# Closing the first expert tile two batch pairs before the end of attention, and rearranging the bridge around it

## The chip, the cores and the metric

The kernel runs on one core of a Trainium2 chip. The core has five engines with instruction queues of their own: TensorE (PE in the profile, with PEld for its weight loads), VectorE (DVE), ScalarE (ACT), GpSimd (POOL) and SyncE (SP, which here only issues transfers). Each queue runs in the order in which it was written, and the engines wait for one another by semaphores. The metric is the time of one execution on the device in microseconds (us), taken as the median over several runs; lower is better.

## The reference

The computation is a sliding-window attention followed by a mixture-of-experts layer without dropped tokens.

```python
# attention: batch 8, heads 8, sequence 576, head size 64, window 64, causal
scores = scale * np.matmul(q, k.transpose(0, 1, 3, 2))
scores = np.where(mask, scores, -1000000000.0)
attn = np.exp(scores - np.max(scores, axis=-1, keepdims=True))
attn = attn / (np.sum(attn, axis=-1, keepdims=True) + 1e-09)
out = np.matmul(attn, v)                      # reshaped to x: 4608 tokens x 512
# experts: 8, hidden size 1024
logits = x @ w_gate
expert_idx = np.argmax(logits, axis=1)        # one expert per token
gate_w = probs[np.arange(N), expert_idx]      # softmax of the logits, its largest entry
for e in range(E):                            # tokens sorted by expert
    h = np.maximum(x_sorted[lo:hi] @ w1[e], 0.0)
    y_sorted[lo:hi] = h @ w2[e]
return gate_w[:, None] * y[inv_perm]
```

So every token goes through one expert, and which one is known only when its attention output and its logits are done.

## The kernel before

**Attention.** The batch is cut into four pairs (`bg` 0 to 3, `last` = 3) and the heads into four pairs, which gives 16 units. A unit has three steps of three 128-token blocks each, so there are N = 48 steps, 0 to 47. `step(s)` writes out one step of a software pipeline by hand: PE computes the scores of step s + 1 into banks 0 and 1 (`scored`, L572), DVE masks them and takes the largest (`masked`, L585), ACT takes the exponentials (`softened`, L595); PE then does the weighted sum over v of step s - 1 in bank 6 (`weighted`, L618), part of the logits of step s - 3 (`logit`, L655), and turns the probabilities of step s (`flipped`, L603), which DVE and ACT copy (L605); DVE divides (`divided`, L628 to L632); PE turns q and k for step s + 3 (`turned`, L531 and L539) and the result of step s - 2 (`x_turned`, L643). Four banks (2 to 5) are handed out in a ring for what is turned. Other work is put behind these with a list, `todo[s]`, whose entries are written out in order at the end of step s.

**Routing.** When a pair's logits are complete, `by_tokens` brings them to token order and `choose(bg)` does the routing in five parts on DVE, with an exponential on ACT and two small matmuls: the largest logit (L686 to L692), the one-hot of the expert (L695, L698, exponential L699), the ranks among the tokens (L705) and the gate (L715 to L717), the running count (L722 to L732), and the position split in a high and a low part (L734 to L742). After that `place(j)` writes two one-hot matrices of the low part for each of the pair's nine blocks on DVE (L746), `weigh` scales a block by its gates (L757 on POOL, L755 on ACT), and `store` writes the result to `x_dram` (L766, L773). For the third pair (`bg` = 2) the function `after` lays this over steps 39 to 44: the five parts in steps 39, 39, 40, 41, 41, the one-hots three to a step in 42 to 44, the scalings in 41 to 44 with two of the nine on ACT, and in step 45 `first_tiles`.

**First tiles.** A tile holds 256 tokens of one expert. The first two tiles of expert 0 (`NE` = 2) are closed before the last pair is routed: `first_tiles` compares the high parts with the slot numbers of both tiles (L859, L862), multiplies the one-hots of 27 blocks in 54 narrow matmuls on PE (L869), takes the slots as token numbers (L872) and gathers tile 0's tokens on POOL (`gather_first`: a clear L280 and an indirect transfer L282 for each half). A count is raised to 512 for expert 0 after the third pair (L730), so that both tiles are padded if there are too few tokens.

**The bridge.** After step 47 the last pair's routing runs on DVE, and tile 0 goes through expert 0 as PE's filling between its parts: `turn` (eight transposes, L303, in banks 2 and 3, copies on ACT), `sums_x` (four DVE operations, L311), then `hidden` and `output` (fourteen block products, L322 and L362, in a Strassen scheme with seven for each layer). Sums of w2's blocks for that scheme are formed on POOL (`sums_w2`, four operations, L139, into the memory that held the turned q and k). `slot_table` builds the remaining slots from all 36 blocks: large comparisons (L799), the last nine blocks' one-hots and 72 narrow matmuls (L807). `next(tile0)` and `next(table)` alternate by hand. Tile 1 follows, then a loop over the experts that is bound by PE.

Memory of the q and k ring is used again: xg, the gathered rows, lies where unit 13's q was, and w2 of expert 0 lies where units 14 and 15 were, so its two halves are loaded from SP as those come free (L919).

Of the kernel before, what the change touches and what calls it, by code (L numbers as in the profile page):

```python
# [12 lines left out]
BF16 = mybir.dt.bfloat16  # L13
# [18 lines left out]
def _inner(ap: bass.AP, n: int) -> bass.AP:  # L32
    return _ins(ap, len(ap.ap), n)
# [3 lines left out]
def kernel(  # L37
# [174 lines left out]
    key = rt.tile([P, NJE], BF16, name="key")  # L212
    hi_e = rt.tile([P, NJE, NE * C], BF16, name="hi_e")
    at_b = rt.tile([P, NJ], BF16, name="at_b")
# [61 lines left out]

    def gather_first(tokens):

        for c in range(C):
            G.memset(xg[c], 0.0)  # L280

            G.indirect_dma_start(  # L282
                out=xg[c], out_offset=None, in_=x_dram[0 : NT - BG * S, :],
                in_offset=bass.IndirectOffsetOnAxis(ap=tokens[:, c : c + 1], axis=0),
                bounds_check=NT - BG * S - 1, oob_is_err=False,
            )
# [11 lines left out]

    def turn():
# [7 lines left out]
    def sums_x():  # L307

        b12, b22, b21 = tps[1][:, 0:HG], tps[1][:, HG:], tps[0][:, HG:]
        for n, (a, b) in enumerate(((b12, xq[:, 0, 0]), (b22, xs[:, 0]), (b22, xq[:, 0, 1]), (xs[:, 1], b21))):  # L310
            V.tensor_tensor(out=xs[:, n], in0=a, in1=b, op=ALU.subtract)  # L311
# [128 lines left out]
    with tc.manual_schedule(), ExitStack() as held, ExitStack() as brief:  # L440
# [236 lines left out]
        def choose(bg):  # L677
# [101 lines left out]
        def slot_table(hi):  # L779
# [53 lines left out]
        def after(s, routing, bg):  # L833
# [13 lines left out]

            for n in (0, 0, 1, 2, 2):
                do(n, part)
            for m in range(NTB):  # L850
                do(3 + m // 3, partial(place, bg * NTB + m))
                do((2, 2, 3, 3, 4, 4, 4, 5, 5)[m], partial(weigh, bg, m, nc.scalar if m in (2, 6) else G))
                if m % ST == ST - 1:
                    do(3 + m // ST, partial(store, bg, m // ST, G))
            do(6, first_tiles)

        def first_tiles():

# [3 lines left out]
            V.tensor_tensor(  # L862
                out=hi_e[:], in0=_inner(key[:], NE * C), in1=_ins(hi_id[:, C + 1 : C + 1 + NE * C], 1, NJE),
                op=ALU.is_equal,
            )
            slots = banks[next(tr_ring)](0, NE * C)
            for j in range(NJE):
                for i in range(2):
                    nc.tensor.matmul(  # L869
                        slots, lhsT=lo[:, i, j], rhs=hi_e[:, j], start=(i + j == 0), stop=(i + j == NJE)  # L870
                    )
            V.tensor_scalar(out=perm_e[:], in0=slots, scalar1=-1.0, scalar2=float(NT), op0=ALU.mult, op1=ALU.add)  # L872
            gather_first(perm_e[:, 0:C])

# [65 lines left out]
        tile0 = chain(hidden(0), turn(), output(0))  # L940
# [12 lines left out]
        next(by_tok[0], None)  # L953
        next(by_tok[1])
# [33 lines left out]
        gather(perm_i[:, 3 * C : 4 * C])  # L988
# [82 lines left out]
```

## Time and profile before

| | us |
|---|---|
| median of 7 runs | 765.42 |
| lowest, highest | 763.85, 766.90 |
| profiled execution, its own time | 764.96 |
| span of that profile | 763.1 |
| PE busy in the span | 721.1 (94%) |
| DVE, ACT, POOL busy | 397.0, 268.1, 357.0 |
| PE busy, 160 to 196 | 34.34 of 36 |
| PE busy, 196 to 214 | 12.94 of 18 |
| PE busy, 214 to 248 | 32.68 of 34 |
| PE busy, 248 to 763 | 491.71 of 515 |

The four stretches are: the steps in which the third pair is routed, the last attention steps, the bridge, and the expert tiles. In an answer in order of time, the columns are start, duration, engine, line, operation, what is written and read, count, and in brackets the idle time just before and what ended it. In the table by windows, the columns after the window are its length and then the busy time (and instructions) of PE, PEld, DVE, ACT and POOL, the granted TensorE clock as a share of the full one, the busy share of the transfer engines, and GB/s.

### The profile page before, as it was taken

Reading aid. Unit: us, or ns where it says so; the run is one execution under the profiler, and the core shown is the slowest. Engines: PE = TensorE matmul, PEld = TensorE weight load, DVE = VectorE, ACT = ScalarE, POOL = GpSimd, SP = SyncE. Lnnn points to the kernel's source line nnn. Section 1 sums busy time; section 2 is a strip of 40 time slices with the busy share of each in tenths; the row PEclk is TensorE's granted clock in tenths of the full one; section 3 lists DMA queues with packets and bytes.
Section 4 is the critical chain, followed back from the end, with each engine's and each line's share of the span. In section 5 each row is a group of like instructions: output and inputs, shape, how many; then the busy total and the mean of one; then the engine's idle time right before and its main releaser. Section 6 shows DMA issues by size and latency. Waiting matters only on the chain. (4 is left out here: it accounts for less than half of the span.)

```text
span 763.1 us, 18401 instructions
## 1 busy us (share of the span) xinstructions
PE 721.1 (94%) x7018; PEld 650.9 (85%) x7018; DVE 397.0 (52%) x1355; ACT 268.1 (35%) x676; POOL 357.0 (47%) x366
## 2 busy tenths in 40 slices
PE   5999999999799999999999999999999999999995
PEld 3888888887688988988999899899988899988994
DVE  2667898988758544523542353352434452424432
ACT  4788888787633201211221122111220121211220
POOL 4215567594760635537531653663256465262111
PEclk9999999999999999999999999999999999999998
DMA  7898889883513712603410260442171171101101
GB/s 158 208 212 190 187 195 253 178 222 122 191 45 125 277 58 61 234 29 136 161 53 33 92 212 29 159 149 70 30 255 46 39 256 56 42 24 42 43 29 53
DMA packets 137620, 94.55 MB, mean 124 GB/s; under 512 B 117072, under 2 KB 117072, under 8 KB 137490
## 3 DMA queue, kind: packets, MB, share of 16 engines
q1 hardware_dynamic: 127858, 62.16, 29.8%
q0 software_dynamic: 9056, 28.58, 11.6%
q10 hardware_dynamic: 576, 2.10, 0.8%
q8 instruction: 78, 1.28, 0.7%
q14 instruction: 52, 0.43, 0.2%
HBM read 73.94 MB, written 20.45 MB: 124 GB/s over the span
## 5 line engine op out<-in xcount | busy, mean ns | idle before, releaser
L322 PE MATMUL bank<-qk_m,s 128*128 128x128 f32 x1216 | 145.3, 275 | 0.0
L322 PEld LDWEIGHTS bank<-qk_m,s 128*128 128x128 f32 x1216 | 140.4, 192 | 0.0
L322 PE MATMUL bank<-qk_m,w 128*128 128x128 f32 x912 | 112.2, 276 | 12.6 <-DVE v_m L358 8.7
L272 POOL DMA_INDIRECT qk_m<-x_dram,at_g x42 | 44.6, 1063 | 168.3 <-PE bank L303 161.0
L322 PEld LDWEIGHTS bank<-qk_m,w 128*128 128x128 f32 x912 | 106.7, 192 | 17.6 <-issue 17.4
L595 ACT ACTIVATE pr<-pr,mx 128x128 f32<-128x128 f32 x288 | 89.7, 390 | 33.7 <-DVE mx L585 33.5
L358 DVE TENSOR_TENSOR v_m<-bank,v_m 128x256 f32<-128x256 f32 x101 | 40.9, 422 | 110.0 <-PE bank L362 54.8
L585 DVE CUSTOM_DVE_ANT_0 pr<-bank,mask 128x128 f32<-128x128 f32 x288 | 64.4, 286 | 27.4 <-PE bank L572 26.0
L329 ACT COPY qk_m<-bank 128x512 f32<-128x512 f32 x19 | 11.1, 586 | 166.0 <-PE bank L322 164.9
L292 POOL DMA_INDIRECT out_dram<-v_m,at_s x42 | 42.4, 1009 | 56.7 <-DVE v_m L358 44.9
L139 POOL TENSOR_TENSOR s<-w 128x1024 f32<-128x1024 f32 x22 | 52.3, 2377 | 18.4 <-DMA qk_m<-x_dram,at_g 14.3
L362 PE MATMUL bank<-qkT_m,v_m 128*128 128x256 f32 x240 | 54.0, 380 | 1.8 <-DVE v_m L139 1.8
L362 PEld LDWEIGHTS bank<-qkT_m,v_m 128*128 128x128 f32 x240 | 45.4, 190 | 8.7 <-DVE v_m L139 2.6
L362 PE MATMUL bank<-qk_m 128*128 128x256 f32 x224 | 52.1, 380 | 0.0
L513 POOL COPY v_m<-v_m 64x520 f32<-64x520 f32 x32 | 19.8, 619 | 68.0 <-DMA v_m<-in_v_dram 59.9
L618 PEld LDWEIGHTS bank<-v_m,pT 128*64 128x64 f32 x1152 | 41.1, 140 | 11.9 <-DVE xs L632 5.7
L618 PE MATMUL bank<-v_m,pT 128*64 128x65 f32 x1152 | 47.8, 231 | 2.9 <-DVE xs L632 2.9
L362 PE MATMUL bank<-s,v_m 128*128 128x256 f32 x216 | 48.1, 379 | 0.0
L572 PE MATMUL bank<-qkT_m 64*64 64x128 f32 x1152 | 46.0, 290 | 0.3 <-DVE mx L585 0.2
L362 PEld LDWEIGHTS bank<-qk_m 128*128 128x128 f32 x224 | 41.5, 190 | 5.5 <-ACT v_m L374 0.4
L362 PEld LDWEIGHTS bank<-s,v_m 128*128 128x128 f32 x216 | 41.0, 190 | 5.6
L539 PE MATMUL bank<-ident,qk_m 128*128 128x128 f32 x256 | 35.9, 283 | 7.9 <-POOL mask L461 4.9
(167 smaller groups left out, 1223.1 us busy)
## 6 DMA issues: line engine op xcount, KB each, us to landing
w<-in_moe_w_dram SPq DMA_DIRECT2D x11, 2048.0 KB, 14.8
qk_m<-in_q_dram SPq DMA_DIRECT2D x72, 128.0 KB, 3.5
qk_m<-in_k_dram SPq DMA_DIRECT2D x72, 128.0 KB, 3.6
v_m<-in_v_dram SPq DMA_DIRECT2D x64, 128.0 KB, 4.1
qk_m<-in_moe_w_dram SPq DMA_DIRECT2D x3, 2048.0 KB, 15.6
x_dram<-xs POOLq DMA_DIRECT2D x6, 512.0 KB, 4.5
x_dram<-xs POOLq DMA_DIRECT2D x3, 768.0 KB, 7.0
w<-in_moe_w_dram ACTq DMA_DIRECT2D x4, 512.0 KB, 4.1
```

The source lines that it names most:

```text
L139: op()
L272: G.indirect_dma_start(out=xg[c], out_offset=None, in_=x_dram[:, :], in_offset=bass.IndirectOffsetOnAxis(ap=at_g[:, c : c + 1], axis=0),)
L292: put = G.indirect_dma_start(out=out[:, :], out_offset=bass.IndirectOffsetOnAxis(ap=at_s[:, c : c + 1], axis=0), in_=ys[c], in_offset=None ...
L322: nc.tensor.matmul(acc[:, f, :], lhsT=a[:, g, f * P : (f + 1) * P], rhs=b[:, g, :], start=(first and f == 0 and g == 0), stop=(g == HG - 1 ...
L358: plus = lambda out, a, b: V.tensor_tensor(out=out, in0=a, in1=b, op=ALU.add)
L362: nc.tensor.matmul(acc, lhsT=a[:, f, :], rhs=b[:, f, :], start=(start and f == 0), stop=(stop and f == HF - 1), skip_group_check=True,)
L513: nc.gpsimd.tensor_copy(out=vb[0:D, i].rearrange("p j h d -> p (j h d)"), in_=va[D:P, i].rearrange("p j h d -> p (j h d)"),)
L539: nc.tensor.transpose(out=tr.rearrange("d a b -> d (a b)").rearrange("d (p j) -> d j p", j=NV)[:, j, :], in_=t[:, c, j].rearrange("p h d - ...
L572: nc.tensor.matmul(out_, lhsT=qT[rows, t, a * WINDOW : (a + 1) * WINDOW], rhs=rhs, start=True, stop=True, skip_group_check=True,)
L585: V.tensor_tensor_reduce(out=prs[h][:, m, :], in0=scs[h][:, m, :], in1=mask[:, m0 + m, :], scale=-scale, scalar=-2 * MASKED, op0=ALU.add, ...
L595: nc.scalar.activation(out=y, in_=y, func=AF.Exp, scale=-1.0, bias=mx[:, h, m : m + 1])
L618: nc.tensor.matmul(px[a * D : (a + 1) * D, h, m, :], lhsT=pTs[h][:, m, a * D : (a + 1) * D], rhs=vt[:, h, :], start=True, stop=True, skip_ ...
```

## The change

The selection of the first tiles is split. `first_tile(0)` works on the 18 blocks of the first two pairs, with its comparison in step 38 and its matmuls and gather in step 39; `first_tile(1)` works on 27 blocks and is written between the products of the bridge. The count of expert 0 is raised to 256 after the second pair and to 512 after the third. Tile 0 is turned in step 46 through banks 0 and 1, and its first product is written in step 47, with the sums of w2 behind it. The third pair's five parts move to steps 39, 40, 40, 41, 42, its one-hots to two each in 43 to 45 and three in 46, its scalings to steps 41 to 45, all on POOL. The loads of w2 stand one step earlier. In the bridge, 54 of the slot table's matmuls come behind the second three one-hots, and the last three scalings with their store come behind the copy of tile 0's first output product.

```diff
-            if bg == last - 1:
+            if last - NE <= bg < last:
-                V.tensor_scalar_max(count[:, 0:1], count[:, 0:1], float(NE * TB))
+                V.tensor_scalar_max(count[:, 0:1], count[:, 0:1], float((bg - last + NE + 1) * TB))
...
-            for j in range(NJE):
-                fill(j)
             for n in range(NST):
                 for m in range(ST):
                     place(NJE + n * ST + m)
+                if n == 1:
+                    for j in range(NJE):
+                        fill(j)
                 yield
...
-            for n in (0, 0, 1, 2, 2):
+            for n in (0, 1, 1, 2, 3):
                 do(n, part)
             for m in range(NTB):
-                do(3 + m // 3, partial(place, bg * NTB + m))
-                do((2, 2, 3, 3, 4, 4, 4, 5, 5)[m], partial(weigh, bg, m, nc.scalar if m in (2, 6) else G))
+                do((4, 4, 5, 5, 6, 6, 7, 7, 7)[m], partial(place, bg * NTB + m))
+                do((2, 3, 3, 4, 4, 5, 5, 6, 6)[m], partial(weigh, bg, m, G))
                 if m % ST == ST - 1:
-                    do(3 + m // ST, partial(store, bg, m // ST, G))
-            do(6, first_tiles)
-        def first_tiles():
+                    do(4 + m // ST, partial(store, bg, m // ST, G))
+        def first_tile(n):
+            nj = (last - NE + n + 1) * NTB
             V.scalar_tensor_tensor(
-                out=key[:], in0=rkhi[:, 0:NJE], scalar=1.0, in1=oh_all[:, 0, 0:NJE], op0=ALU.add, op1=ALU.mult
+                out=key[:, 0:nj], in0=rkhi[:, 0:nj], scalar=1.0, in1=oh_all[:, 0, 0:nj], op0=ALU.add, op1=ALU.mult
             )
...
+            yield
+            slots = banks[next(tr_ring)](0, C)
+            for j in range(nj):
                 for i in range(2):
                     nc.tensor.matmul(
...
+            to = perm_e[:, n * C : (n + 1) * C]
+            V.tensor_scalar(out=to, in0=slots, scalar1=-1.0, scalar2=float(NT), op0=ALU.mult, op1=ALU.add)
+            gather_first(to, nj * P)
+            yield
...
-        for n, s in enumerate((N - 6, N - 3)):
+        for n, s in enumerate((N - 7, N - 4)):
...
+        tile0 = chain(hidden(0), turn(), output(0))
+        first = first_tile(0)
+        todo.setdefault(N - 10, []).append(partial(next, first))
+        todo.setdefault(N - 9, []).append(partial(next, first))
+        free = [banks[i](0, NG, P) for i in (0, 1)]
+        todo.setdefault(N - 2, []).extend((lambda: form_all(turn(free)), partial(sums_x, free)))
+        todo.setdefault(N - 1, []).extend((partial(next, tile0), partial(sums_w2, 0)))
         for s in range(-3, N):
             step(s)
-        sums_w2(0)
...
         px = weighted(N - 1, pTs.pop(N - 1))
-        form_all(turn())
         logit(N - 3)
         divided(N - 1, px)
         x_turned(N - 2)
-        sums_x()
-        gather_first(perm_e[:, C : 2 * C])
+        second = first_tile(1)
+        next(second)
+        next(tile0)
         by_tok = [by_tokens(last, c) for c in range(NST)]
         next(by_tok[0])
-        next(tile0)
         logit(N - 2)
         x_turned(N - 1)
+        next(second)
...
         weigh_some(1)
-        next(tile0)
         next(routing, None)
-        weigh_some(2)
         next(tile0)
...
-        for _ in range(8):
+        for n in range(8):
             next(tile0)
             next(table, None)
+            if n == 1:
+                weigh_some(2)
```

More of the change, by code (lines that the diff above doesn't have):

```diff
@@ L212 @@
     key = rt.tile([P, NJE], BF16, name="key")
-    hi_e = rt.tile([P, NJE, NE * C], BF16, name="hi_e")
+    hi_e = rt.tile([P, NJE, C], BF16, name="hi_e")
     at_b = rt.tile([P, NJ], BF16, name="at_b")
@@ L275, in gather, with gather_first @@
             )
-    def gather_first(tokens):
+    def gather_first(tokens, rows):
         for c in range(C):
@@ L282, in gather_first @@
             G.indirect_dma_start(
-                out=xg[c], out_offset=None, in_=x_dram[0 : NT - BG * S, :],
+                out=xg[c], out_offset=None, in_=x_dram[0:rows, :],
                 in_offset=bass.IndirectOffsetOnAxis(ap=tokens[:, c : c + 1], axis=0),
-                bounds_check=NT - BG * S - 1, oob_is_err=False,
+                bounds_check=rows - 1, oob_is_err=False,
             )
@@ L297, in scatter, with turn @@
             tc.add_to_no_dep_group("puts", put.ins)
-    def turn():
+    def turn(tps=tps):
         for c in range(C):
@@ L305, in turn, with sums_x @@
         yield
-    def sums_x():
+    def sums_x(tps=tps):
         b12, b22, b21 = tps[1][:, 0:HG], tps[1][:, HG:], tps[0][:, HG:]
@@ L846, in after @@
                 return
-            for n in (0, 0, 1, 2, 2):
+            for n in (0, 1, 1, 2, 3):
                 do(n, part)
             for m in range(NTB):
-                do(3 + m // 3, partial(place, bg * NTB + m))
-                do((2, 2, 3, 3, 4, 4, 4, 5, 5)[m], partial(weigh, bg, m, nc.scalar if m in (2, 6) else G))
+                do((4, 4, 5, 5, 6, 6, 7, 7, 7)[m], partial(place, bg * NTB + m))
+                do((2, 3, 3, 4, 4, 5, 5, 6, 6)[m], partial(weigh, bg, m, G))
                 if m % ST == ST - 1:
-                    do(3 + m // ST, partial(store, bg, m // ST, G))
-            do(6, first_tiles)
-        def first_tiles():
+                    do(4 + m // ST, partial(store, bg, m // ST, G))
+        def first_tile(n):
+            nj = (last - NE + n + 1) * NTB
             V.scalar_tensor_tensor(
-                out=key[:], in0=rkhi[:, 0:NJE], scalar=1.0, in1=oh_all[:, 0, 0:NJE], op0=ALU.add, op1=ALU.mult
+                out=key[:, 0:nj], in0=rkhi[:, 0:nj], scalar=1.0, in1=oh_all[:, 0, 0:nj], op0=ALU.add, op1=ALU.mult
             )
             V.tensor_tensor(
-                out=hi_e[:], in0=_inner(key[:], NE * C), in1=_ins(hi_id[:, C + 1 : C + 1 + NE * C], 1, NJE),
-                op=ALU.is_equal,
-            )
-            slots = banks[next(tr_ring)](0, NE * C)
-            for j in range(NJE):
+                out=hi_e[:, 0:nj], in0=_inner(key[:, 0:nj], C),
+                in1=_ins(hi_id[:, (n + 1) * C + 1 : (n + 2) * C + 1], 1, nj), op=ALU.is_equal,
+            )
+            yield
+            slots = banks[next(tr_ring)](0, C)
+            for j in range(nj):
                 for i in range(2):
                     nc.tensor.matmul(
-                        slots, lhsT=lo[:, i, j], rhs=hi_e[:, j], start=(i + j == 0), stop=(i + j == NJE)
+                        slots, lhsT=lo[:, i, j], rhs=hi_e[:, j], start=(i + j == 0), stop=(i + j == nj)
                     )
-            V.tensor_scalar(out=perm_e[:], in0=slots, scalar1=-1.0, scalar2=float(NT), op0=ALU.mult, op1=ALU.add)
-            gather_first(perm_e[:, 0:C])
+            to = perm_e[:, n * C : (n + 1) * C]
+            V.tensor_scalar(out=to, in0=slots, scalar1=-1.0, scalar2=float(NT), op0=ALU.mult, op1=ALU.add)
+            gather_first(to, nj * P)
+            yield
         N = NU * NST
@@ L934 @@
         assert not todo
-        sums_w2(0)
         tr_ring = cycle((4, 5))
-        tile0 = chain(hidden(0), turn(), output(0))
         px = weighted(N - 1, pTs.pop(N - 1))
-        form_all(turn())
         logit(N - 3)
```

## The prediction

> **What bounds the kernel now.** Times are us from the start of the span, unless a sum says otherwise. The page first: PE is busy 94% of 763.1 us, and only a bridge, between the attention steps and the expert loop, has holes that the diff can reach. I then read the two-microsecond windows from 180 to 262, the waits of PE, and the order of time on PE, DVE and POOL there.
>
> ```profile
> 200.00:202.00 2.00, 0.38 (x4) 0.20 (x3) 1.97 (x16) 1.44 (x5) 1.71 (x2) 1.00 0.17 68
> 202.00:204.00 2.00, 0.93 (x37) 0.93 (x37) 0.95 (x4) 1.15 (x4) 2.00 (x4) 1.00 0.47 131
> 204.00:206.00 2.00, 2.00 (x49) 1.65 (x45) 0.16 (x1) 0.00 (x0) 0.08 (x1) 0.65 0.85 274
> 206.00:208.00 2.00, 2.00 (x32) 1.57 (x30) 1.35 (x12) 1.55 (x6) 0.79 (x1) 0.50 0.00 0
> 208.00:210.00 2.00, 1.27 (x12) 0.97 (x9) 1.28 (x4) 1.18 (x4) 1.73 (x3) 1.00 0.44 117
> ```
>
> PE (first pair after the window's length) stands nearly still from 200.4 to 203.1 and then runs at a granted clock of 0.65 and 0.50 for some 4 us (third value from the end).
>
> ```profile
> 188.06 0.55 PE L643 MATMUL bank<-ident,xs 128*128 128x128 f32 x3 [1.41 <-DVE pT L605]
> 203.07 1.49 PE L869 MATMUL bank<-hi_e,lo 128*128 128x4 bf16 x54 [2.70 <-DVE hi_e L862]
> 204.50 1.52 PE L572 MATMUL bank<-qkT_m 64*64 64x128 f32 x24
> 213.49 0.97 PE L618 MATMUL bank<-v_m,pT 128*64 128x65 f32 x24 [0.88 <-DVE xs L632]
> 240.05 1.91 PE L807 MATMUL bank<-hi,lo 128*128 128x62 bf16 x54 [1.29 <-DVE qk_m L311]
> 247.06 0.69 PE L807 MATMUL bank<-hi,lo 128*128 128x62 bf16 x18
> ```
>
> The releaser is DVE nearly each time. 213.49 is the weighted sum of the last step, 47: from there the last pair's routing starts. 247.06 are the last slots; tile 1's first product follows at 247.58 and PE is then full. So the change is worth what it moves 247.58.
>
> ```profile
> 192.98 0.81 DVE L746 TENSOR_SCALAR lo<-lane,low,tok_b 128x128 bf16<-128x128 bf16 x1
> 233.80 0.69 DVE L139 TENSOR_TENSOR v_m<-qk_m 128x512 f32<-128x512 f32 x1 [0.67 <-ACT qk_m L350]
> 261.82 2.84 DVE L139 TENSOR_TENSOR v_m<-qk_m 128x512 f32<-128x512 f32 x1 [0.76 <-ACT qk_m L350]
> ```
> ```profile
> 191.29 0.82 POOL L766 DMA_DIRECT2D x_dram<-xs  x1 [8.08 <-issue]
> 192.16 4.71 POOL L757 TENSOR_SCALAR xs<-xs,gate 128x512 f32<-128x512 f32 x3
> 210.19 2.36 POOL L139 TENSOR_TENSOR qkT_m<-qk_m 128x1024 f32<-128x1024 f32 x1
> ```
>
> These decide my forecast. A DVE subtraction takes 0.69 us alone and 2.84 while POOL runs its own L139; a one-hot takes 0.31 alone, 0.81 beside POOL's scalings (three tokens' pairs of them: 2.41 us from 192.76 to 195.17, against 1.34 alone). POOL idles 8.08 us before 191.29, and its sums of w2 run at 210.19, after all of the third pair's one-hots.
>
> **The change part by part.** The chip's later work is the same: by the reference's inputs expert 0 has 421 tokens in two pairs (256 needed) and 538 in three (512 needed), so no tile is padded.
>
> *Step 45's selection goes.* Off PE: the 2.70 wait, its 54 narrow matmuls (1.43, 203.07 to 204.50) and the half clock (scores 1.45 for 0.81, weighted sum 1.55 for 0.90, logits 0.57 for 0.35: 1.5). Together 5.6 us.
>
> *Tile 0's selection in steps 38 and 39.* 36 matmuls of 27 ns, 1.0 us, on a PE without a hole there. DVE's three small operations (0.2 each, by L859, L862, L872) lie beside it. POOL: two clears of 0.55 and two gathers of about 1.07 with 0.27 before each, 3.8 us, behind the copies that end at 179.06. So the scalings start at 182.9 instead of 180.10. The gather lands 3.4 us later, twenty before step 46 wants it.
>
> *Turn and first product in steps 46 and 47.* 1.04 and 1.88 us of PE move ahead of 213.49; tile 0's own work is not changed in sum. The turn must wait for the masking of step 47's scores (same banks 0, 1) and the product for all four sums of x (L311, 1.53).
>
> *Choosing one part per step.* In step 40 the gate now waits for an exponential that stands behind ACT's copy ending at 180.41: 180.41 + 0.27, then 0.73 of gate: masking starts at 181.45, was 180.34. Each step takes DVE 1.27 masking + 0.47 copy + 0.88 division = 2.62. To step 45's one-hots are five of these, 13.1, with part four (1.41), part five (1.28) and four one-hot pairs (0.89 + 0.89): 17.6 alone, so they are asked for at 199.0. But POOL, idle there before, now scales all nine blocks from 182.9 (the two that were ACT's, 0.74 each, too, which spares ACT nothing it lacked): 9 x 1.56 + stores 0.82 + 1.32 + 1.92 + 0.3 before each = 19.0, to 202.0. With two operations in 0.8, as in the 2.41 row, these extras become 2.4 + 2.3 + 1.6 + 1.6 and the one-hots are asked for at 202.5. Bounds 199.0 and 202.5; I take the middle, 200.8, as stores and gaps between scalings let operations through.
>
> *Sums of w2.* Nothing ties them to DVE. The first two write the half of qkT_m that step 44's scores released, the others need step 47's; so they follow the stores: 202.0 to 211.45 (4 x 2.36) instead of 210.19 to 219.6. Queued behind them on POOL is only tile 1's gather, landing about 222, wanted about 230. The loads of w2, on SP a step earlier, wait there for PE's turned blocks as before (the first went out at 178.51, the second some 14 us later), and their 6.5 us to landing end before 204.4, when the second sum reads them. If step 45's one-hots pass by 201.7, masking ends at 203.0, turn at 204.1, copies at 204.75, sums of x at 206.4: step 46's six one-hot operations meet the sums. Low end: the scalings' row, 2.4 us, to 208.8. High end: L139's row, a full POOL operation each time, so two pass at 206.7, two at 209.1, two at 211.45: 211.9. I take the high end, since the POOL instruction is that of L139; another short two-input operation, L695, took 0.77 instead of 0.23 until POOL's L919 sum had ended. Copy and division (1.35) and a start of 0.05 make the last weighted sum 213.3; 213.5 with POOL stretched (L139 2.36 to 2.79 in the contended stretch). No earlier than before. PE then waits from about 208.3 for 5 us, more than the 2.70 that halved the clock, with the routing chain behind: 1.5 (above) to 2.0 (4 us at half), I take 1.7.
>
> The Trainium skill, page "SBUF — State Buffer", section "Who interferes with whom", says that the one to issue second fully blocks until the other finishes. The L139 row agrees (2.84), the L746 row beside scalings (0.81 under a 1.56 us operation) does not quite; by the rule the sum is the 766.0 below, by that row 760.3, so the rule speaks against the change.
>
> *The tail.* From the last weighted sum to the last logits: 9.85 before (213.49 to 223.34); the turn leaves (1.02), 54 narrow matmuls come (1.43): 10.26. From there DVE bounds, 24.08 to the last one-hot's end (247.42). Its waits of 0.67 (relu behind scalings, which move behind the copy) and 0.91 (a sum for PE) close and one addition (0.61) now lies earlier: 21.9. Bounds: 24.1 if the waits come back, 21.9. I take 21.9: DVE is late there, PE has one product less to cover it with, so the waits are PE's, at the last slots, instead of the old 1.29. Net -1.8. The moved fill of 54 costs nothing under DVE's one-hots; the later store of the last scalings goes out on SP some 10 us before the gather that reads it.
>
> *Sum.* Last weighted sum +0.0, clock +1.7, tail -1.8: -0.1. If step 45's one-hots (asked at 202.5) meet the sums instead: they end at 207.2, masking 208.4, turn and copies 210.2, sums of x 211.75, one-hots 213.1, weighted sum 214.5 to 214.9, +1.2, with a half-speed turn +1.0, tail -1.8: +0.4, to +2 with small delays. I take +0.6 over both. The profiled run took 764.96 (1.86 round the span of 763.1), 0.46 under the median of 765.42; the shift goes on the median: **766.0**.
>
> **The rivals.** *One-hots slip between the sums* (low end): last weighted sum at 210.2, -3.3; the hole of 1.9 us lies between 1.41 (clock kept) and 2.70 (lost); tail -1.8: -5.1, 760.3; half of it 762.5. For: the same DVE instruction in the 0.81 row. Against: L139, L695.
>
> *Parts four and five are blocked for whole scalings* (slower): most of their eleven operations have two inputs in SBUF like L139. At up to 1.56 each, part four ends by 193 instead of 186, and the masking behind it makes PE wait in step 42 already. Every further us is lost 1:1 once step 45's one-hots come after 202.0. Price: from 0 to 8 us on top of the main case; its middle, 4: 770.0. For: the same DVE operation class as L139. Against: the scalings' own row shows only half an operation of delay.
>
> *The change adds nothing at all*: excluded by the matmuls and waits above.
>
> **How the numbers follow.** Main case 0.46 (764.5 to 768), slip 0.30, whole scalings 0.20, something unseen 0.04. A measurement here can tell about 0.2%, 1.5 us, from no change. Main case: 0.05 faster, 0.26 same, 0.15 slower; slip faster 0.29, same 0.01; whole scalings slower 0.20; the rest split. Faster 0.36, same 0.27, slower 0.37. The range of 8 in 10 reaches into both rivals: 760.3 to 769.8.
>
> **What would show it.** Right: no narrow matmuls near 203; POOL scaling without a hole from 183; L139 on POOL from about 202; L746 rows of 1 to 2.4 us in step 46; last weighted sum near 213.5, a clock near 0.5 behind it, next product near 248. Wrong: L746 rows of at most 0.8 under L139 and the last weighted sum at 211 or earlier (faster), or L726 to L742 rows of 1.5 and holes in steps 42 to 44 (slower).
>
> The Trainium skill, page "TensorE: Matmul & The Clock Gate", Part 1, says that about 3.4 us of busy time release the full clock; the windows above show some 4. By its figure the loss would be an estimate of 1.7, as taken.

## The result, and the profile after

The changed kernel took 768.40 us in the median of 19 runs (766.59 to 770.24), against 765.71 us for the kernel before in 45 runs beside them. The ratio is 1.0035, with a 95% interval from 1.0027 to 1.0044: slower by about 2.7 us. Measured once more later, beside other kernels, it was 768.90 us and 1.0039 (1.0025 to 1.0053). The forecast was 766.0 us, with a range from 760.3 to 769.8.

The profiled execution took 768.15 us, with a span of 766.2. Not all of the 3.1 us by which this span is longer than the 763.1 before belongs to the change: step 38's copy of the turned probabilities (line 605) is the last landmark that the diff leaves alone, and it already starts at 174.83 instead of 173.23. Over the thirteen profiles of this study, whose code up to there differs by one short operation on DVE at most (the count that is raised after the second pair, 0.15 us), it starts anywhere from 172.33 to 175.51. So kernels are compared below by a stretch that is called the *bridge* from here on, though it begins earlier than the work behind step 47: the time from that copy to the first hidden product behind the slot table (line 322). It was 74.35 us before (247.58 less 173.23) and is 75.80 us after (250.63 less 174.83): +1.45. Numbers that are called "aligned" have the 1.60 us by which step 38 starts later taken off.

The windows of two microseconds, after; the columns are the window, its length, the busy time of PE, PE's weight loads, DVE, ACT and POOL with their instructions, then the granted clock, the DMA share and GB/s:

```profile
204.00:206.00 2.00, 2.00 (x38) 1.73 (x37) 2.00 (x3) 0.01 (x1) 1.92 (x2) 1.00 0.33 100
206.00:208.00 2.00, 0.33 (x4) 0.10 (x1) 2.00 (x2) 0.00 (x0) 2.00 (x2) 1.00 0.00 0
208.00:210.00 2.00, 0.00 (x0) 0.00 (x0) 2.00 (x2) 0.00 (x0) 2.00 (x2) 1.00 0.00 0
210.00:212.00 2.00, 1.42 (x8) 1.06 (x8) 1.93 (x16) 1.87 (x7) 2.00 (x1) 0.83 0.03 8
212.00:214.00 2.00, 1.68 (x26) 1.44 (x24) 0.78 (x2) 1.70 (x4) 0.62 (x2) 0.50 0.00 0
214.00:216.00 2.00, 2.00 (x22) 1.50 (x19) 1.97 (x8) 0.34 (x1) 0.00 (x0) 0.81 0.00 0
216.00:218.00 2.00, 1.69 (x16) 1.50 (x14) 1.90 (x7) 0.75 (x3) 0.00 (x0) 1.00 0.00 0
```

The hole at 200.4 to 203.1 is gone, and a wider one has opened at 206.3 to 210.6. In it PE and ACT stand, while DVE is busy all the time with two instructions in each window, beside a POOL that is busy all the time too. An engine that is full with so few instructions, of a kind that takes 0.31 us alone, has instructions that are stretched. The order of time on POOL and DVE shows them (start, duration, engine, line and operation, with the idle time before it and its releaser in brackets):

```profile
183.93 4.67 POOL L757 TENSOR_SCALAR xs<-xs,gate 128x512 f32<-128x512 f32 x3
...
202.67 2.38 POOL L139 TENSOR_TENSOR qkT_m<-qk_m 128x1024 f32<-128x1024 f32 x1
205.13 2.42 POOL L139 TENSOR_TENSOR qkT_m<-qk_m,qkT_m 128x1024 f32<-128x1024 f32 x1
207.50 2.33 POOL L139 TENSOR_TENSOR qkT_m<-qk_m 128x1024 f32<-128x1024 f32 x1
209.80 2.35 POOL L139 TENSOR_TENSOR qkT_m<-qkT_m,qk_m 128x1024 f32<-128x1024 f32 x1
```

```profile
200.57 0.31 DVE L746 TENSOR_SCALAR lo<-lane,low,tok_a 128x128 bf16<-128x128 bf16 x1
...
203.64 1.47 DVE L746 TENSOR_SCALAR lo<-lane,low,tok_a 128x128 bf16<-128x128 bf16 x1
205.03 0.30 DVE L746 TENSOR_SCALAR lo<-lane,low,tok_b 128x128 bf16<-128x128 bf16 x1
205.25 2.34 DVE L746 TENSOR_SCALAR lo<-lane,low,tok_a 128x128 bf16<-128x128 bf16 x1
207.51 2.38 DVE L746 TENSOR_SCALAR lo<-lane,low,tok_b 128x128 bf16<-128x128 bf16 x1
209.81 0.28 DVE L585 CUSTOM_DVE_ANT_0 pr<-bank,mask 128x128 f32<-128x128 f32 x1
```

The four sums of w2 begin at 202.67. Step 45's four one-hots come to DVE 0.97 us later. Of an instruction that takes 0.31 us alone, the first ends with the first sum, one slips through, and the next two end with the second and the third sum. The four take 6.2 us instead of 0.9, and step 47's masking stands behind them on DVE until 209.81. Its first results release PE, whose order of time is:

```profile
205.84 0.49 PE L643 MATMUL bank<-ident,xs 128*128 128x128 f32 x3
210.58 1.67 PE L303 MATMUL bank<-ident,qk_m 128*128 128x128 f32 x8 [4.24 <-DVE mx L585]
212.56 1.62 PE L618 MATMUL bank<-v_m,pT 128*64 128x65 f32 x24 [0.32 <-DVE xs L632]
...
218.02 0.97 PE L618 MATMUL bank<-v_m,pT 128*64 128x65 f32 x24 [0.33 <-DVE xs L632]
...
243.98 1.90 PE L807 MATMUL bank<-hi,lo 128*128 128x62 bf16 x54
...
249.25 1.54 PE L807 MATMUL bank<-hi,lo 128*128 128x62 bf16 x18
250.63 2.03 PE L322 MATMUL bank<-qk_m,w 128*128 128x128 f32 x16
```

PE's 4.24 us wait stands in the place of the old 2.70. The last weighted sum starts at 218.02, 43.19 us behind step 38's copy; before it was 40.26. From there to the next hidden product it is 32.61 us; before it was 34.09 (213.49 to 247.58). So the change loses 2.93 us ahead of the last weighted sum and wins back 1.48 behind it.

Second profiles of both kernels gave nearly the same: 74.08 us before (39.98 and 34.10), 75.89 us after (43.27 and 32.62).

### The profile page after: what moved, and what is told of

Its sections match the earlier page's. It is cut to its first block, busy times and chain, and to the rows that moved or that the text cites. A ratio compares the mean times of both kernels' runs of the same rounds, so it can differ in the third digit from the quotient of the medians.

```text
span 766.2 us, 18486 instructions
## 1 busy us (share of the span) xinstructions
PE 722.9 (94%) x7054; PEld 651.7 (85%) x7054; DVE 402.7 (53%) x1359; ACT 267.0 (35%) x674; POOL 361.2 (47%) x368
## 5 line engine op out<-in xcount | busy, mean ns | idle before, releaser
L139 POOL TENSOR_TENSOR s<-w 128x1024 f32<-128x1024 f32 x22 | 52.3, 2376 | 18.3 <-DMA qk_m<-x_dram,at_g 13.8
```

What stands on the lines that cost most here:

```text
L139: op()
```

## The experiments

The theory after the first look: the sums of w2 stretch step 45's one-hots, and that alone turns a gain into a loss. The rivals: GpSimd's scalings, which now fill steps 42 to 45, do the harm; or the lower granted clock behind the hole does; or something in the whole program does that the bridge does not show.

**The sums left out.**

```diff
-todo.setdefault(N - 1, []).extend((partial(next, tile0), partial(sums_w2, 0)))
+todo.setdefault(N - 1, []).append(partial(next, tile0))
```

> The changed kernel without the four sums of w2 on POOL (the products read what lies there, so the output is not the reference's). Theory: the sums, which begin at 202.7 under step 45's one-hots, hold DVE 5.4 us (rows of 1.47, 2.34 and 2.38 instead of 0.31) and cost the clock after a PE hole of 4.2 us. Then without them the four rows are 0.31 each, the hole in front of the turn falls below 0.5, the last weighted sum comes 5 to 6.5 us earlier and the time is 762 to 763.5, against 768.4 changed and 765.7 before. Rival: the scalings that now run under the routing parts four and five are the main cost (part five took 3.1 us instead of 1.3): then the time stays at 767 or more.

Measured: 763.5 us, ratio 0.9964 (0.9946 to 0.9981), at the upper end of what was expected. Step 45's one-hots take 0.31 us each and the 4.24 us wait is absent from the list of PE's waits between 150 and 262 (total, times, longest):

```profile
PE bank L643 <- DVE pT L605: 2.3, 2, 1.2
PE bank L705 <- DVE oh_all L695: 0.7, 2, 0.5
PE bank L618 <- DVE xs L632: 0.6, 1, 0.6
PE bank L322 <- DVE qk_m L311: 0.4, 1, 0.4
```

The bridge is 70.81 us, with the last weighted sum at 38.18. So in the changed kernel the sums cost 5.0 us (75.80 less 70.81), all of it ahead of the last weighted sum, and everything else in the change together gains 3.5 us on the first profile of before.

**The sums held behind the last one-hots.** A copy of one column makes GpSimd wait for step 46's last one-hot.

```diff
+mark = consts.tile([P, 1], BF16, name="mark")
...
+        def held_sums():
+            G.tensor_copy(out=mark[:], in_=lo[:, 1, last * NTB - 1, 0:1])
+            sums_w2(0)
+
-        todo.setdefault(N - 1, []).extend((partial(next, tile0), partial(sums_w2, 0)))
+        todo.setdefault(N - 1, []).extend((partial(next, tile0), held_sums))
```

> The sums of w2 truly behind the third pair's one-hots: a copy on POOL of one element column of the last one-hot stands ahead of them, so that they start when step 46's one-hots are done. Theory: as without the sums up to the last weighted sum; the sums run from about 209 to 218.5, and the two small two-input operations of the second selection may wait up to 2.4 us there: 762.5 to 765. Rival (scalings): 767 or more. If the sums meet something of the tail that nobody listed: above 766 with one-hots at 0.31.

Measured: 766.22 us, ratio 1.000 (0.9982 to 1.0018), above the expected 762.5 to 765: the place behind the last one-hots is not free either. The one-hots are free, and the last weighted sum lies at 38.90, close to the 38.18 without the sums. But the sums now run from 210.05 to 219.44, and the next short operations in DVE's queue meet them (the lines of this kernel are one higher):

```profile
213.14 1.74 DVE L861 SCALAR_TENSOR_TENSOR key<-rkhi,oh_all 128x27 bf16<-128x27 f32 x1
214.92 2.29 DVE L864 TENSOR_TENSOR hi_e<-key,hi_id 128x54 bf16<-128x54 bf16 x1
...
217.26 1.50 PE L872 MATMUL bank<-hi_e,lo 128*128 128x2 bf16 x54 [1.62 <-DVE hi_e L864]
...
218.82 3.45 PE L323 MATMUL bank<-qk_m,w 128*128 128x128 f32 x16
```

Tile 1's selection, some 0.4 us of DVE's work when nothing is beside it, takes 4.1 us, from 213.14 to 217.21. PE waits 1.62 us for it and the product behind it runs 3.45 us instead of 1.98, at a granted clock of 0.62 and 0.52 in the windows from 218 to 222. From the last weighted sum to the next hidden product it is 35.97 us, 3.4 more than after: the 1.62 and the 1.47 of the slowed product are 3.1 of that.

**The one-hots pulled forward**, three in each of steps 42 to 44, so that the sums should find none left.

```diff
-                do((4, 4, 5, 5, 6, 6, 7, 7, 7)[m], partial(place, bg * NTB + m))
+                do((3, 3, 3, 4, 4, 4, 5, 5, 5)[m], partial(place, bg * NTB + m))
```

> The changed kernel with the third pair's one-hots back at three a step in steps 42 to 44, so that the sums find none of them. Theory: nine one-hots under the scalings at 0.8 each instead of 0.45 cost DVE some 3 us in steps 42 to 44, but the hole of 4.2 us and the half clock go: 764 to 766. Rival (scalings are the main cost): one-hots all under scalings, 769 or more.

Measured: 773.17 us, ratio 1.009 (1.0062 to 1.0117), bridge 80.68. A clear miss. DVE was late in step 44 already, and the sums came at 202.46 as ever:

```profile
202.27 2.62 DVE L746 TENSOR_SCALAR lo<-lane,low,tok_a 128x128 bf16<-128x128 bf16 x1
204.81 0.30 DVE L746 TENSOR_SCALAR lo<-lane,low,tok_b 128x128 bf16<-128x128 bf16 x1
205.03 2.33 DVE L746 TENSOR_SCALAR lo<-lane,low,tok_a 128x128 bf16<-128x128 bf16 x1
207.28 2.38 DVE L746 TENSOR_SCALAR lo<-lane,low,tok_b 128x128 bf16<-128x128 bf16 x1
```

```profile
210.79 2.19 PE L572 MATMUL bank<-qkT_m 64*64 64x128 f32 x24 [5.92 <-DVE mx L585]
```

The last three pairs, now in step 44, met the sums there (the first of them begins, by the record, 0.19 us ahead of the first sum, while GpSimd still issues a store, and yet ends with that sum; these rows do not say what held it so early): the block moved one step further from the end, and the fourth sum then waited 3.58 us for the scores that use its buffer. The position of the sums against *all* of DVE's short work decides, not against one step's.

**PE kept busy in the hole.** 32 transposes of the identity, which nothing uses, ahead of the turn; they fill most of the hole, so that the clock stays up. A second run has 16.

```diff
+        def filler():
+            t = banks[next(tr_ring)](0, NG, P)
+            for n in range(32):
+                nc.tensor.transpose(out=t[:, n % NG, :], in_=ident[:], identity=ident[:])
+
+        todo.setdefault(N - 2, []).append(filler)
```

> The changed kernel with 32 transposes of the identity, read by nobody, on PE in step 46 ahead of the turn, where PE waits 4.2 us. It prices the clock alone: the rows of the turn, the weighted sum and the logits took 1.67, 1.62 and 0.65 at a granted clock of 0.5 to 0.83 instead of 1.04, 0.97 and 0.42. Theory: they go back to full speed, and 1 to 1.5 us of that is on the path: 767.0 to 767.4. If the clock is not on the path there (the sums of x and the one-hots on DVE end last anyway): 768.2 to 768.6.

Measured: 777.61 us, ratio 1.0143 (1.0115 to 1.0172), far outside. In its profile the bridge is 76.31 us, 0.5 more than after, and the granted clock is 1.00 from 196 to 230:

```profile
205.19 3.66 PE L945 MATMUL bank<-ident 128*128 128x128 f32 x32
209.67 1.29 PE L303 MATMUL bank<-ident,qk_m 128*128 128x128 f32 x8 [0.82 <-DVE mx L585]
211.66 0.97 PE L618 MATMUL bank<-v_m,pT 128*64 128x65 f32 x24 [0.70 <-DVE xs L632]
...
217.12 0.97 PE L618 MATMUL bank<-v_m,pT 128*64 128x65 f32 x24 [0.58 <-DVE xs L632]
```

This answers the question of the clock. From the turn to the last weighted sum it is 7.45 us here, at full clock (209.67 to 217.12), and 7.44 us after, at a granted clock down to 0.50 (210.58 to 218.02). The turn and step 46's weighted sum are 0.38 and 0.65 us longer after, and neither moves the end. A chain through ScalarE and DVE sets it: the copies of the turn (L304) stand in ScalarE's queue behind six exponentials and two other copies, and DVE waits 1.22 us for them in both kernels before its sums of x, its one-hots, its copy and its division. In the changed kernel:

```profile
210.13 1.87 ACT L595 ACTIVATE pr<-pr,mx 128x128 f32<-128x128 f32 x6 [6.13 <-DVE mx L585]
212.63 1.07 ACT L304 COPY qk_m<-bank 128x512 f32<-128x512 f32 x2
213.73 1.21 DVE L311 TENSOR_TENSOR qk_m<-bank,qk_m 128x256 f32<-128x256 f32 x3 [1.22 <-ACT qk_m L304]
```

PE, slow as it was, still had the 0.33 us to spare for which it waits ahead of 218.02. What the slow clock cost in the changed kernel, once the hole was there, is nothing that can be seen.

The rest of the 9 us lies where nothing was edited, in the loop over the experts. There PE idles without anything in the profile that releases it ("issue"):

```profile
439.24 3.25 PE L322 MATMUL bank<-qk_m,w 128*128 128x128 f32 x16 [3.97 <-issue]
...
496.64 2.68 PE L322 MATMUL bank<-qk_m,w 128*128 128x128 f32 x16 [3.41 <-issue]
```

> The changed kernel with 16 transposes of the identity that nothing uses ahead of the turn in step 46, where 32 were put earlier (777.6 us, with two waits of 3.97 and 3.41 us at 435 and 493 us, in the loop over the experts, that no engine releases). Theory (those waits come from where TensorE's code behind the bridge comes to lie, not from the transposes' work): the long waits are gone or at other bodies of the loop, and the time is not half way; without them 767 to 769 us. Rival (the time grows with the transposes): half way between 768.4 and 777.6, 773 us, with waits of about 2 us at the same places.

Measured with 16: 777.06 us, ratio 1.0144 (1.0108 to 1.0179), bridge 75.81. The clock fell there, to 0.50 in the window from 212 to 214, PE did not wait ahead of its last weighted sum, and from the turn to it is 7.70 us: a slow PE that has nothing left to spare costs 0.25. Half of the added work, the same time; and the waits lie at other passes of the loop:

```profile
306.15 2.83 PE L322 MATMUL bank<-qk_m,w 128*128 128x128 f32 x16 [3.51 <-issue]
...
363.58 1.72 PE L322 MATMUL bank<-qk_m,w 128*128 128x128 f32 x14 [2.04 <-issue]
```

So the time does not grow with the transposes, against the rival, and it did not fall to 767 to 769 either, against the number that was written for the theory. That these waits follow where PE's code behind the bridge comes to lie fits both runs, but was only argued: nothing here changed the place of the code alone. The reading of the clock rests on the bridge, not on the total.

**The sums behind tile 1's selection.** Selection (key and hi_e) is put ahead of the last division, where DVE waits for the last weighted sum, and the sums start behind hi_e.

```diff
-        todo.setdefault(N - 1, []).extend((partial(next, tile0), partial(sums_w2, 0)))
+        todo.setdefault(N - 1, []).append(partial(next, tile0))
...
         px = weighted(N - 1, pTs.pop(N - 1))
+        second = first_tile(1)
+        next(second)
+        G.tensor_copy(out=mark[:], in_=hi_e[:, NJE - 1, 0:1])
+        sums_w2(0)
         logit(N - 3)
         divided(N - 1, px)
         x_turned(N - 2)
-        second = first_tile(1)
-        next(second)
         next(tile0)
```

> Tile 1's selection on VectorE (key and hi_e) is put ahead of the turn for the last scaling of the attention, and the sums of w2 start on GpSimd behind hi_e, so they meet neither the last one-hots nor the selection. Theory (what the sums cost is VectorE's short operations that cannot run beside them): against the kernel whose sums start behind the last one-hots (766.2 us), key and hi_e fall from 1.74 and 2.29 us to about 0.5 each, the wait of 1.62 us at the selection's products goes, and the product behind it, which took 3.45 us there, takes its usual 1.98: 762.5 to 764 us, ratio 0.995 to 0.9985, next product of tile 0's second half (line of the hidden products, behind the table) at about 244.5 us. Rival (the time does not follow from who meets the sums, it is set by clock and code place): 766 us like the kernel with held sums, or more.

Measured: 764.34 us, ratio 0.998 (0.9958 to 1.0002), 0.3 us above the expected stretch, and the interval just reaches 1. Its bridge, 70.57 us, agrees with the 70.81 without any sums, and the next hidden product came at 244.71. Key and hi_e took 0.18 and 0.22 us. Placed there, the four sums of 2.35 us run from 212.59 to 222.00 and cost nothing in the bridge, and DVE's addition from a bank beside them (line 333 there, at 215.75) takes 0.69 us, as long as line 339's behind them.

**Two scalings back on ScalarE**, on top of that.

```diff
-                do((2, 3, 3, 4, 4, 5, 5, 6, 6)[m], partial(weigh, bg, m, G))
+                do((2, 3, 3, 4, 4, 5, 5, 6, 6)[m], partial(weigh, bg, m, nc.scalar if m in (2, 6) else G))
```

> As the kernel with the sums behind the selection, but the scalings of chunks 2 and 6 of the last but one pair go back to ScalarE, as in the kernel before. Theory (GpSimd's scalings in steps 42 to 44 stretch parts four and five from 1.4 and 1.3 us to 2.0 and 3.1 us and the first one-hots from 0.9 to 1.8, and TensorE waits for the copy behind them, 1.23 us at 195.4): GpSimd ends its scalings about 3.1 us earlier, the waits for the copies of the turned rows fall by about 1 us, and the time is 0.5 to 1.2 us below the kernel with the sums behind the selection. Rival (the waits are for ScalarE, which then has two more scalings of 0.65 us in these steps): the time is the same within 0.5 us or up to 1.3 us longer.

Measured: 763.39 us, ratio 0.9963 (0.9941 to 0.9984), as expected 0.95 us under the version with nine scalings on GpSimd; its bridge is 69.23 us, 1.34 less. The waits of PE between 150 and 262:

```profile
PE bank L619 <- DVE xs L633: 1.4, 3, 0.6
PE bank L706 <- DVE oh_all L696: 0.7, 2, 0.5
PE bank L323 <- DVE qk_m L312: 0.4, 1, 0.4
PE bank L644 <- DVE pT L606: 0.4, 1, 0.4
```

The waits for the copies of the turned probabilities fall from 2.0 us (in two) to 0.4, those for the division rise from 0.6 to 1.4. The reason is not the earlier end of the scalings that was expected: GpSimd waits 5 us for ScalarE, whose scaling runs at 191.31, and ends its stores at 204.8, later than with nine. The hole in GpSimd's work lies where part five runs: its three operations of 9 elements take 0.17 us each instead of 0.7 to 0.8. From one masking to the next, the step with part five is 1.59 us shorter and the one with part four 0.45, while the two steps with the first one-hots are 0.66 longer together: that is the whole gain.

The same version measured again, on one chip with the changed kernel:

> The version with the sums of w2 behind tile 1's selection and two scalings on ScalarE once more (763.4 us, ratio 0.9963 with the interval 0.9941 to 0.9984). Theory (its stretch from step 38 to the next hidden product is 69.23 us, 5.1 us shorter than before, in any execution): 761.5 to 763.5 us, ratio 0.9935 to 0.9975, and 5 us below the changed kernel on the same chip. Rival (the first measurement was lucky): 764.5 us or more, no difference from before.

Measured: 761.37 us, ratio 0.9931 (0.9908 to 0.9954), just below the expected stretch, bridge 69.16, some 7.5 us under the changed kernel beside it. It beats both kernels.

**The changed kernel again, and the kernel before.**

> The changed kernel once more, for a second profile and beside the best version on one chip. Theory (in the first profile 1.6 of the 3.1 us by which its span is longer arose before the first moved instruction, and belong to the execution, not to the change): the stretch from the flip of step 38 to the next hidden product behind the table is 75 to 76.5 us again (75.80 in the first profile, 74.35 before), with the step's own start anywhere in the 172.3 to 175.2 us that the other profiles show; step 45's one-hots again meet the sums of w2. Rival (the early part is longer for the change as well, by where code and tiles lie): step 38 again at about 174.8 us or later. 768.4 us, ratio 1.002 to 1.005.

> The kernel before once more, for a second profile of the stretch that all the comparisons are made against: from the flip of step 38 to the next hidden product behind the table it took 74.35 us (173.23 to 247.58). If that stretch is a property of the kernel, it is 74.2 to 74.6 us again, and the change's own price in it is the 1.45 to 1.54 us of its two profiles. If it varies by a microsecond or more, for instance 73 to 73.5 us, the first profile of before was a slow draw there, and the rest of the 2.7 us between the medians lies in this stretch too.

Measured: 768.90 us, bridge 75.89 after, with the one-hots blocked again and a 4.45 us wait; 764.62 us in one run and bridge 74.08 before, just under the expected 74.2 to 74.6. So the change's price in the bridge is 1.45 to 1.8 us, and repeats. Step 38's copy started at 175.51 and 173.53; for the changed kernel that is outside what the theory allowed, and where the rival put it. The two profiles of the changed kernel are among the three latest of thirteen there. But the code ahead of that copy does not make it late by itself: the ten profiles with the changed code have it at 172.33 to 175.51, 174.2 in the mean, the three with the code of before at 173.23, 173.53 and 175.21, 174.0 in the mean. Behind the bridge the two kernels take the same, 515.2 to 516.2 us to the end of the span. Whether the late starts of the changed kernel are chance or belong to it is not settled, and one to two microseconds of the 2.7 to 3.3 between the medians are not placed by these profiles.

**The tail's edits alone**, put into the kernel before: the moved fill and the moved scalings.

```diff
-            for j in range(NJE):
-                fill(j)
...
+                if n == 1:
+                    for j in range(NJE):
+                        fill(j)
...
-        weigh_some(2)
...
+            if n == 1:
+                weigh_some(2)
```

> The kernel before with the tail's edits of the change alone: the products of the early chunks of the table are formed behind the second group of one-hots, and the last three scalings stand behind the copy of that step. Theory (the tail gives about 2 us, from 24.08 us between the last logits and the last one-hot before to 21.5 us after): 763.2 to 764.4 us, ratio 0.996 to 0.998, and no wait of 1.29 us ahead of the table's products. Rival (the scalings ran beside work that sets the end anyway, and the gain after came from the second selection's move): 765.4 to 766.4 us, as before.

Measured: 765.13 us, ratio 0.9985 (0.9964 to 1.0006): between the two expected stretches, and the interval holds the theory and no change. The profile is clearer: from the last weighted sum to the next hidden product 32.42 us instead of 34.09, a gain of 1.67, and the 1.29 us wait ahead of the table's products is gone.

All bridges beside the medians (us):

```
kernel                         bridge   to last weighted sum   from there   median   ratio
before                   74.35, 74.08           40.26, 39.98        34.09   765.71
after                    75.80, 75.89           43.19, 43.27        32.61   768.40   1.0035
sums left out                   70.81                  38.18        32.63   763.5    0.9964
sums behind one-hots            74.87                  38.90        35.97   766.22   1.000
one-hots pulled forward         80.68                  48.05        32.63   773.17   1.009
32 unused transposes            76.31                  43.69        32.62   777.61   1.0143
16 unused transposes            75.81                  43.22        32.59   777.06   1.0144
sums behind selection           70.57                  37.93        32.64   764.34   0.998
and two scalings on ACT  69.23, 69.16           36.58, 36.50        32.65   763.39   0.9963
tail alone, on before           73.32                  40.90        32.42   765.13   0.9985
```

The part behind the last weighted sum is the same to 0.06 us in seven of these kernels: once the last weighted sum has started and no sum blocks the selection, everything to the slot table follows as by a clock.

## Why the prediction was right or wrong

The median lies 2.4 us above the forecast, inside the range, 0.4 us outside the main case's own, and on the side that had the chance 0.37. The main mechanism was named: short operations on DVE held back by GpSimd's sums take the place of the old wait. That the number came out no further off is in part luck: the last weighted sum came 2.9 us later than before instead of 0.0, and the 1.7 us that were set down for the clock, of which nothing was seen, made up for more than half of that. Point by point:

- *Step 45's selection goes, 5.6 us.* No narrow matmuls and no 2.70 us wait remain there. With the tail's 1.5 us the two gains would make 7.1 us of bridge, and without the sums the kernel gained 3.5. Of the other 3.6, the masking behind the third pair's gate already starts 1.6 us later (183.52, aligned 181.92, against 180.34): tile 0's selection and the gate's wait of 1.11 us for its exponential lie there, and the prediction had 1.1 of it. The scalings' block is 1.3 (the gain of the last version), and the rest was not measured by itself.
- *Tile 0's selection, scalings from 182.9, stores to 202.0.* Right in kind, and early by a little: 183.93 aligned is 182.3, and the sums begin at 202.67, aligned 201.1, where the prediction had 202.0.
- *The request of step 45's one-hots: the step that failed.* The prediction bounded it by 199.0 and 202.5 and took the middle, 200.8, "as stores and gaps between scalings let operations through". It came at 203.64, aligned 202.0. The contended bound was the nearer one. It put 2.4 + 2.3 + 1.6 + 1.6 = 7.9 us for part four, part five and the two sets of one-hots; from the start of each to the masking behind it they took 1.9, 2.9, 1.4 and 0.9, 7.1 in all, 0.8 more than the 6.3 that the middle stands for. The other 0.5 us is the start, a masking at 181.9 aligned instead of 181.45. With 200.8 against 202.0 these one-hots passed ahead of the sums; in fact they came 0.97 us behind the start of the first. One request 1.2 us later and the other 0.9 us earlier than foreseen turned the order round, and the order decided.
- *Which one-hots meet the sums.* The prediction took step 46's, under which PE has the last weighted sum as its only loss, and got a last weighted sum at 213.5. It was step 45's, and 216.4 aligned. The prediction had priced this second path: masking by 208.4, last weighted sum at 214.5 to 214.9, +1.0 for a half-speed turn, +0.4 to +2 in all. The bridge's +1.45 to +1.8 falls in there, though not by that path's own terms. The masking begins at 208.2 aligned instead of 207.2. From there to the sums of x the path has 3.0 us (to 210.2), and it took 3.9 (209.81 to 213.73): the prediction let the turn's copies follow the turn at once, and in ScalarE's queue they stand behind the step's exponentials and two copies. It is 3.9 us in the kernel without the sums too (204.64 to 208.57), so the main case lacked the same 0.9. In return the 1.0 for a half-speed turn was not lost. The weight of this path in the forecast, +0.6 over both, was too small.
- *Full blocking beside L139.* Right: 2.34 and 2.38 us, and 1.47 for the one that came in the middle of a sum. The prediction let two operations pass at each end of a sum; two did at the first, one at each of the others, so the one-hots ended at 209.9, aligned 208.3, where the second path had 207.2. The rival in which the one-hots slip through, 0.30, is refuted by the same rows. The Trainium skill, page "SBUF — State Buffer", section "Who interferes with whom", says that the instruction that comes second stands for the whole of the first; these rows agree with it, those beside the scalings (0.39 to 0.96 us in step 43 under operations of 1.56) only in part.
- *The clock, +1.7.* Not seen. The main case had this loss behind the last weighted sum. The hole came before the turn instead, and from 216 on the granted clock was 1.00 again. Ahead of that it did fall, to 0.83, 0.50 and 0.81 in the windows from 210 to 216, but filling the hole kept it up and left the 7.4 us behind the turn as they were. The slow PE cost nothing here because it still had 0.33 us to spare. Where it has none, the loss is real: with the sums held behind the one-hots, the slowed product costs 1.47 us behind a wait of 1.62.
- *The tail, -1.8.* Right: -1.48, and -1.67 alone. From the last logits to the last one-hot it was 21.72 us (228.82 to 250.54), against the 21.9 foreseen and 24.08 before; from the last weighted sum to the last logits 10.80 instead of 10.26, which is the missing 0.3 and more.
- *Parts four and five are blocked for whole scalings* (770.0, 0.20). Partly true: in part four one operation took 0.84 instead of 0.23 (L731), in part five three in a row took 0.7 to 0.8, and lifting GpSimd's work from there gained 1.3 us of bridge in the last version. That is a half-block, not the whole one of 1.56, and the total stayed 1.6 us below the rival's.

These are the three rows of part five, after, in DVE's order of time; alone each takes 0.17 us:

```profile
191.44 0.77 DVE L740 CAST rkhi<-r_half 128x9 f32<-128x9 int32 x1
192.25 0.70 DVE L741 TENSOR_SCALAR r_half<-r_pos 128x9 int32<-128x9 int32 x1
192.98 0.77 DVE L742 CAST low<-r_half 128x9 f32<-128x9 int32 x1
```

## What to carry to other kernels

When work is moved to GpSimd in a stretch where VectorE issues many short operations, list what will be in VectorE's queue during the whole of it, not only the operations that the edit is about: each one can last as long as GpSimd's instruction beside it, and the next step's masking stands behind them. Follow a chain through the queue of every engine in it: a copy that is written behind a turn starts behind what its engine has to do first, here six exponentials. If the order of two requests decides the outcome and their times are known to a microsecond only, price both orders with near equal weight, or tie the order by a dependency, as the sums behind tile 1's selection do. An experiment that adds instructions to an engine is read in the stretch that it changes; its total may carry something from far behind it.

## What the runs showed that was not expected

- 16 or 32 unused transposes ahead of tile 0's turn made the program about 9 us longer, mostly by waits without a releaser in the loop over the experts: 9.0 us in all for 32 and 7.6 for 16, against 1.3 after, and at other passes of it for 16 than for 32. The cause is open.
- A full clock was worth nothing behind a hole of 4.24 us: 7.45 against 7.44 us from the turn to the last weighted sum. With 16 transposes, when PE was slow and had nothing to spare, it was 7.70.
- Beside GpSimd's scalings, three operations of only 9 elements a partition took 0.70 to 0.77 us instead of 0.17, like those of 128 elements (0.39 to 0.96); beside the sums the selection's operation of 54 elements took 2.29 us instead of 0.22. In these rows the length follows the operation beside, not the size of the short one.
- The time from the step that all these kernels share to their 39th step varies by 3 us between executions (172.33 to 175.51), while the bridge of one kernel repeats to 0.3 us. For differences under half a per cent the aligned stretch told more than the medians of a dozen runs.
